# Tail scores and last-key value products of two head pairs in 64x64 quarters of TensorE's array

## The chip, the core and the metric

The kernel runs on one core of a Trainium2 chip. The metric is the device time of one execution in microseconds (us), as the median of several runs; lower is better. The engines are TensorE (PE, matmuls; PEld are its weight loads), VectorE (DVE), ScalarE (ACT), GpSimd (POOL) and SyncE (SP), which here issues nearly all DMAs from one queue in program order.

## What is computed

Attention of 8 sequences with 8 heads, 576 tokens and head size 64, in which weights below a threshold of the row's maximum are dropped, and behind it a feed-forward layer with an ELU, all in fp32:

```python
scores = scale * np.matmul(q, k.transpose(0, 1, 3, 2))          # (8, 8, 576, 576)
thresh = np.max(scores, axis=-1, keepdims=True) - tau
scores = np.where(scores >= thresh, scores, -1000000000.0)
attn = np.exp(scores - np.max(scores, axis=-1, keepdims=True))
attn = attn / (np.sum(attn, axis=-1, keepdims=True) + 1e-09)
x = np.matmul(attn, v)                                          # to (4608, 512)
h = x @ w_in                                                    # (4608, 2048)
g = np.where(h > 0.0, h, np.exp(np.minimum(h, 0.0)) - 1.0)
out = g @ w_out                                                 # (4608, 512)
```

## The kernel before

**Pairs and steps.** The 64 heads are worked on as 32 pairs of heads, since two heads of 64 fill the 128 partitions. 576 tokens are 4 chunks of 128 (`NC = 4`, together `MAIN = 512`) and a tail of 64 (`TAIL`). A pair takes five steps: steps 0 to 3 handle 128 queries of both heads, step 4 (`i == NC`) handles the 64 tail queries of both heads at once. `steps` (line 529) lists all (pair, step). A step computes scores into PSUM (`scores`, line 220), their maximum (`max_of`), exponentials on ScalarE (`exp_of`), the thresholded weights with their sum (`mask_of`, VectorE) and the normalized weights `w` (`normalize`, GpSimd).

**Scores.** In a full step each head is one row half of the array: 64 rows, 128 columns, twice 288 keys. In the tail step both heads are one matmul with 128 rows: the tail queries stand in a block-diagonal tile `qd`, which `copy_q` (line 200) fills on GpSimd from `qT`.

**The turn of the weights.** The value product needs `w` with keys on partitions. `turn_squares` (line 375) turns squares of 32 on VectorE into `x`, and SyncE writes `x` to a DRAM tile `there` (line 393, four DMAs). `fetch` (line 397) reads it back in the turned order into `wTa` (steps 0 and 1) or `wTb` (steps 2, 3 and the tail; lines 401 and 403). `wTa` and `wTb` have one buffer each. Step n is turned while step n+1 runs and fetched while step n+2 runs. The nine chunks of a turned step are 4 of the first head, one that both heads share (the last 64 keys of each), and 4 of the second head.

**Values.** `values` (line 408) makes one half of a pair's output: part 0 from `wTa`, part 1 from `wTb`. First one matmul over the whole array for the last keys of both heads (line 416: block-diagonal `vd`, chunk `NC`), then eight with 64 columns each (line 420: `vm`, the two heads in the two column halves). They add up in `pv`, a tile of the one bank of pool `t`. `values_out` (line 424) copies `pv` on ScalarE to `xt`, the feed-forward layer's input, and the tail tokens to DRAM.

**The third stage.** From pair 9 on (`MIDDLE`, line 854) the stage in question runs: attention of one batch beside the feed-forward layer of the one before, which uses a scheme of seven block products in place of eight. PSUM holds three banks for it (pool `f`), two score buffers of two banks (pool `s`) and one bank of pool `t`. Its unit on TensorE is a quarter of four matmuls, `ffn_quarters` (line 1176). The program order of every engine comes from a planned clock: `on_pe` (line 918) puts a piece on TensorE and moves the clock by a planned cost; `at(t, f)` puts work of other engines at a planned time. The times are only a plan that sorts instructions, and on the chip every engine works through its own list in order and waits on semaphores.

**Order within a pair.** I call the position of a step in its pair its place. The loop at line 1235 does, for each place: the fetch of step n-2 (planned 1.5 us into the place), `softmax` of the step (line 1194), then quarters, values and quarters. `QUARTERS` (line 1233) gives 8, 6, 4, 6 and 4 quarters to places 0 to 4. Part 1 of the pair ahead follows the quarters of place 2, part 0 of the running pair those of place 4 (`values_of(*steps[n - 3])`). `softmax` also plans loads and turns of q and k for later pairs: VectorE turns the raw tile `qm` in place 0 (`prep_q`, line 192), after which four DMAs load k into the same buffer (line 176); place 2 turns k and loads q; place 3 loads v.

## Time and profile before

| quantity | value |
|---|---|
| median of three runs (lowest, highest) | 1368.72 us (1367.94, 1369.15) |
| profiled execution: span from first to last instruction | 1366.1 us |
| granted TensorE clock | 0.994 |
| scores of pair 10's and pair 30's place 0 | 345.2 and 1065.1 us |
| places 0 to 4 of the pair at 705.19 us | 8.28, 6.55, 7.81, 6.24, 7.03 us |
| share of the 16 DMA engines, 400 to 1,100 us | 86.3% |
| VectorE and GpSimd busy in that pair of 35.91 us | 32.74 and 24.45 us |

How to read the lines of the profile: a group names the source line, the engine, the operation, the tiles (output<-inputs), the shape, and how many there were; then busy time, mean ns of one, and idle time ahead of it. A timeline row gives the start in us from the span's start, the length of the merged run, and what ran. A DMA row on SPq is the time in which SyncE issued it; its landing is told apart. `64*128` are rows and columns of the array that a matmul uses. `sc` are scores, `pv` values, `f` the feed-forward banks. An fp32 matmul of the program shows as two records.

### The profile page before, as it was taken

What the parts mean: (1) busy time and instruction counts of PE and PEld (TensorE: products, weight loads), DVE (VectorE), ACT (ScalarE), POOL (GpSimd) and SP (SyncE); (2) the same over time, 40 slices, a digit from 0 to 9 for tenths busy, and PEclk for the clock granted to TensorE, in tenths of its full rate; (3) what the DMA queues carried; (4) which work ended last, traced back from release to release, by engine and by line L of the source; (5) the groups of instructions that cost most, each with busy time, mean ns of one, the idle gap of its engine ahead of it and who ended that gap; (6) DMA issues with size and microseconds to landing.
All of it is one profiled execution on the core that took longest, in us unless ns stands there. A gap on an engine that the chain in (4) does not pass through costs nothing.

```text
span 1366.1 us, 22394 instructions
## 1 busy us (share of the span) xinstructions
PE 1340.4 (98%) x6796; PEld 1008.9 (74%) x6796; DVE 1064.7 (78%) x2344; ACT 638.5 (47%) x1418; POOL 825.2 (60%) x1322
## 2 busy tenths in 40 slices
PE   8998999999999999999999999999999999999998
PEld 7665746747777777777777777777777777888886
DVE  6879895988888887888798978888898875445433
ACT  5777675226354445545453636363636452412320
POOL 4657673878657574757475747675675646525423
PEclk9999999999999999999999999999999999999999
DMA  5254451688888989798889888897889785412211
GB/s 116 59 108 137 132 151 43 198 247 256 237 251 239 260 229 259 206 267 247 230 234 263 236 238 241 245 269 203 245 225 266 218 258 155 135 59 66 93 59 31
DMA packets 316343, 259.84 MB, mean 190 GB/s; under 512 B 208320, under 2 KB 272320, under 8 KB 316224
## 3 DMA queue, kind: packets, MB, share of 16 engines
q1 hardware_dynamic: 313856, 258.13, 67.6%
q8 instruction: 54, 0.88, 0.3%
q10 hardware_dynamic: 2368, 0.30, 0.2%
q14 instruction: 65, 0.53, 0.1%
HBM read 167.84 MB, written 90.51 MB: 189 GB/s over the span
## 4 chain that ended last, share of the span: by engine, by line
PE 89%; DVE 4%; ACT 2%; POOL 2%; issue 1%; DMA 0%; ACTq 0%; DVEq 0%; POOLq 0%; SPq 0%
PE f L1110 28%; PE f L955 28%; PE sc L236 13%; PE pv L420 9%; PE f L507 3%; PE rt L306 3%; PE pv L416 3%; PE f L467 2%; DVE mx L276 1%; POOL w L272 1%; DVE w L296 1%; ACT e L287 1%; DVE wtop L142 0%; ACT wTa L322 0%; DVE wtop L137 0%
## 5 line engine op out<-in xcount | busy, mean ns | idle before, releaser
L272 POOL TENSOR_SCALAR w<-w,rs 128x576 f32<-128x576 f32 x288 | 248.4, 867 | 120.7 <-DVE rs L303 99.9
L276 DVE TENSOR_REDUCE mx<-sc 128x1 f32<-128x576 f32 x270 | 192.8, 750 | 89.0 <-PE sc L236 88.8
L296 DVE SCALAR_TENSOR_TENSOR w<-sc,th,e 128x576 f32<-128x576 f32 x270 | 212.8, 811 | 26.7 <-ACT e L287 10.0
L287 ACT ACTIVATE e<-sc,nb,keep 128x576 f32<-128x576 f32 x270 | 223.0, 831 | 9.2 <-POOL nb L612 0.7
L285 ACT ACTIVATE nb<-mx,nkeep 128x1 f32<-128x1 f32 x254 | 75.2, 296 | 256.4 <-DVE mx L276 256.4
L380 DVE STREAM_TRANSPOSE x<-w 128x512 f32<-128x512 f32 (+1 forms) x350 | 182.6, 568 | 8.2 <-POOL w L272 8.2
L236 PE MATMUL sc<-kT,qT 64*128 64x288 f32 x1024 | 166.7, 431 | 9.0 <-DVE w L296 6.1
L236 PEld LDWEIGHTS sc<-kT,qT 64*128 64x128 f32 x1024 | 92.8, 187 | 71.4 <-issue 49.4
L280 POOL TENSOR_SCALAR th<-mx,ntau 128x1 f32<-128x1 f32 x270 | 75.7, 281 | 114.0 <-DVE mx L276 113.3
L955 PE MATMUL f<-xt,sw 128*128 128x256 f32 x512 | 128.9, 389 | 0.5 <-DVE g L977 0.5
L955 PE MATMUL f<-xt,w_in_sb 128*128 128x256 f32 x512 | 124.5, 382 | 0.3 <-ACT w L969 0.2
L955 PEld LDWEIGHTS f<-xt,sw 128*128 128x128 f32 x512 | 93.3, 190 | 28.9 <-issue 13.5
L955 PEld LDWEIGHTS f<-xt,w_in_sb 128*128 128x128 f32 x512 | 96.1, 190 | 18.9 <-ACT xs L432 4.6
L1110 PE MATMUL f<-w_out_sb,s 128*128 128x256 f32 x448 | 109.4, 387 | 0.0
L1110 PE MATMUL f<-w_out_sb,g 128*128 128x256 f32 x448 | 107.6, 382 | 0.5 <-DVE g L1010 0.5
L1110 PE MATMUL f<-t,s 128*128 128x256 f32 x448 | 106.6, 380 | 0.3 <-POOL s L1047 0.3
L955 PE MATMUL f<-x,w_in_sb 128*128 128x256 f32 x448 | 105.8, 379 | 0.0
L1110 PEld LDWEIGHTS f<-w_out_sb,s 128*128 128x128 f32 x448 | 82.3, 190 | 23.0 <-issue 11.3
L1110 PEld LDWEIGHTS f<-w_out_sb,g 128*128 128x128 f32 x448 | 83.8, 190 | 16.9 <-issue 4.2
L974 POOL TENSOR_TENSOR u<-u,w 128x256 f32<-128x256 f32 x64 | 48.9, 764 | 76.5 <-ACT u L969 76.5
L1110 PEld LDWEIGHTS f<-t,s 128*128 128x128 f32 x448 | 84.1, 190 | 13.7 <-POOL s L1047 2.7
L955 PEld LDWEIGHTS f<-x,w_in_sb 128*128 128x128 f32 x448 | 85.1, 190 | 11.6
(165 smaller groups left out, 2435.4 us busy)
## 6 DMA issues: line engine op xcount, KB each, us to landing
there<-x SPq DMA_DIRECT2D x500, 144.0 KB, 4.2
wTb<-there SPq DMA_DIRECT2D x75, 576.0 KB, 4.9
wTa<-there SPq DMA_DIRECT2D x50, 576.0 KB, 4.3
sw<-win_sums SPq DMA_DIRECT2D x62, 384.0 KB, 4.6
t<-wout_sums SPq DMA_DIRECT2D x45, 512.0 KB, 5.6
qm<-in_q_dram SPq DMA_DIRECT2D x128, 72.0 KB, 4.2
vm<-in_v_dram SPq DMA_DIRECT2D x64, 128.0 KB, 4.3
wst<-in_moe_w_in_dram SPq DMA_DIRECT2D x16, 512.0 KB, 4.3
```

The source lines that it names most:

```text
L236: nc.tensor.matmul(scs[h][:, a, :HALF], qs[r], kT[r, k0 : k0 + HALF], start=True, stop=True)
L272: nc.gpsimd.tensor_scalar(wv, wv, st["rs"][:, h : h + 1], 1.0, ALU.mult, ALU.mult)
L276: nc.vector.tensor_reduce(st["mx"][:, h : h + 1], st[h][:, :, :HALF], axis=AX.XY, op=ALU.max)
L280: nc.gpsimd.tensor_scalar(st["th"][:, h : h + 1], st["mx"][:, h : h + 1], 1.0, ntau, ALU.mult, ALU.add)
L285: nc.scalar.mul(st["nb"][:, h : h + 1], st["mx"][:, h : h + 1], nkeep)
L287: nc.scalar.activation(e, st[h][:, :, :HALF], AF.Exp, bias=st["nb"][:, h : h + 1], scale=keep)
L296: nc.vector.scalar_tensor_tensor(wv, sc[:, :, :HALF], st["th"][:, h : h + 1], e, ALU.is_ge, ALU.mult, accum_out=st["sm"][:, h : h + 1])
L380: nc.vector.transpose(x[:, :, c0 : c0 + nc_], src.rearrange("p (c g n) -> p g c n", c=nc_, n=T))
L420: nc.tensor.matmul(pv[h * D : (h + 1) * D, g0 * T : g1 * T], vm[:, h, c], wT[:, g0:g1, h * (NC + 1) + c], start=False, stop=(c == NC - 1), ...
L955: nc.tensor.matmul(loc["banks"][place], left[:, j], right[:, j], start=(begins and j == 0), stop=(j == 1), skip_group_check=True)
L974: nc.gpsimd.tensor_tensor(loc[name], x(), loc[other], op)
L1110: nc.tensor.matmul(place(m), lhs, rhs, start=(begins and v == 0), stop=(v == RU - 1), skip_group_check=True)
```

## The change

From pair 9 on (`JOINED`), the steps of a pair run in the order 0, 1, tail, 2, 3, so the tail stands in place 2. In that place a new function, `tails_and_values`, issues two things together: the tail scores of the running pair, as four matmuls of 64 rows and 64 columns (each head on its own, without `qd`), and the last-key products of the pair ahead, also as four 64x64 matmuls, two for each half of the output. The four positions of the array are shared so that in each round head 0's scores, head 0's last keys, head 1's scores and head 1's last keys have one quarter each. The remaining products of both parts (`values_main`) follow at once, and then the place's quarters. `pv` is now a tile of two banks from the score pool `s`. The values of the last pair come by themselves at the end (`last_values`).

The tail's turn now has five chunks for each head instead of nine for both: one turn of 128x512 and two of 64 keys for two chunks, four writes, and two reads instead of one. `copy_q` is no longer called in this stage. The fetch in place 2 is planned at 3.4 us instead of 1.5. `QUARTERS` becomes 7, 6, 2, 7 and 6, all behind the values.

```diff
--- before.py
+++ after.py
@@ -308,10 +308,10 @@
 
 
     def turned_tile(pr, i):
-        if i in (0, 2):
-            n = (2 if i == 0 else 3) * NT
-            wTs[pr, i // 2] = wtp.tile([P, n, NCH, T], FP32, name="wTb" if i else "wTa")
-        return wTs[pr, min(i // 2, 1)], i % 2 * NT + (NT // 2 if i >= 2 else 0)
+        part = int(i >= 2)
+        if (pr, part) not in wTs:
+            wTs[pr, part] = wtp.tile([P, (2 + part) * NT, NCH, T], FP32, name="wTb" if part else "wTa")
+        return wTs[pr, part], i % 2 * NT + (NT // 2 if part else 0)
 
 
     def turn_parts(pr, i):
@@ -383,6 +383,19 @@
             turn_part(0, w[:, :MAIN], NC)
             turn_part(NC, w[:, MAIN : MAIN + P], 1)
             turn_part(NC + 1, w[:, MAIN + P :], NC)
+        elif pr >= JOINED:
+            turn_part(1, w[:, :MAIN], NC)
+            tail = w[:, MAIN:S].rearrange("p (g n) -> p g n", n=T).unsqueeze(1).broadcast_to([P, 2, 2, T])
+            for g in (0, 2):
+                nc.vector.transpose(x[:, g : g + 2, :: NC + 1].rearrange("p g c n -> p c g n"), tail)
+            there = turns[pr, i] = dram.tile([NT, T, NT, (NC + 1) * T], FP32, name="there")
+            for p in range(NT):
+                h = int(p < 2)
+                nc.sync.dma_start(
+                    there[:, :, (p + 2) % NT].rearrange("c k n -> k c n"),
+                    x[p * T : (p + 1) * T, :, 1 - h : NC + 2 - h].rearrange("k c j n -> k c (j n)"),
+                )
+            return
         else:
             turn_part(0, w[:, :MAIN], NC)
             turn_part(NC + 1, w[:, :MAIN], NC)
@@ -399,6 +412,13 @@
         wT, g0 = turned_tile(pr, i)
         if i < NC:
             nc.sync.dma_start(wT[:, g0 : g0 + NT].rearrange("p g c n -> p g (c n)"), back)
+        elif pr >= JOINED:
+            for h in range(2):
+                g = h * (3 * NT - 2)
+                nc.sync.dma_start(
+                    wT[:, g : g + 2, h * NC : h * NC + NC + 1].rearrange("p g c n -> p g (c n)"),
+                    back[:, 2 * h : 2 * h + 2],
+                )
         else:
             nc.sync.dma_start(
                 wT.rearrange("p (a b) c n -> p a b (c n)", b=2)[:, ::5],
@@ -421,6 +441,46 @@
                                  start=False, stop=(c == NC - 1), skip_group_check=True)
         return lambda: values_out(pr, part, pv)
 
+    def tails_and_values(pr, before):
+
+        pv = parts = None
+        if pr is not None:
+            qT, kT, _ = pairs[pr]
+            st = open_steps[pr, NC] = {x: small.tile([P, 2], FP32, name=x) for x in ("mx", "nb", "th", "sm", "rs")}
+            sc = st[0] = psum["s"].tile([P, 2, 512], FP32, name="sc")
+        if before is not None:
+            b, j = divmod(before, NPAIR)
+            vm, vd = (raws[before][x] for x in ("vm", "vd"))
+            parts = [wTs.pop((before, part)) for part in range(2)]
+            if b not in xts:
+                xts[b] = xpool.tile([P, KJ, MAIN], FP32, name="xt")
+            pv = psum["s"].tile([P, 2, 512], FP32, name="pv", tag="sc")
+
+        def span(h, part):
+            return (2 * h, 2 * h + 10) if part else (0, 2 * NT)
+
+        for a in range(2):
+            for h in range(2):
+                r, x = slice(h * D, (h + 1) * D), a ^ h
+                if pr is not None:
+                    nc.tensor.matmul(sc[D - h * D : P - h * D, x, :HALF], qT[r, MAIN:],
+                                     kT[r, TAIL + x * HALF : TAIL + (x + 1) * HALF], start=True, stop=True,
+                                     skip_group_check=True)
+                if before is not None:
+                    g0, g1 = span(h, x)
+                    nc.tensor.matmul(pv[r, x, g0 * T : g1 * T], vd[r, r], parts[x][r, g0:g1, NC],
+                                     start=True, stop=False, skip_group_check=True)
+
+        def values_main(part):
+            for c in range(NC):
+                for h in range(2):
+                    g0, g1 = span(h, part)
+                    nc.tensor.matmul(pv[h * D : (h + 1) * D, part, g0 * T : g1 * T], vm[:, h, c],
+                                     parts[part][:, g0:g1, h * (NC + 1) + c], start=False, stop=(c == NC - 1),
+                                     skip_group_check=True)
+
+        return values_main, [lambda part=part: values_out(before, part, pv[:, part]) for part in range(2)]
+
     def values_out(pr, part, pv):
         b, j = divmod(pr, NPAIR)
         q0, n = TAIL * part, (3 if part else 2) * NT * T
@@ -526,8 +586,9 @@
 
     NP = B * NPAIR
     NB = NC + 1
-    steps = [(pr, i) for pr in range(NP) for i in range(NB)]
     per_seq = NPAIR * NB
+    JOINED = (2 * NPAIR + 1)
+    steps = [(pr, i) for pr in range(NP) for i in ((0, 1, NC, 2, 3) if pr >= JOINED else range(NB))]
 
     def behind(pr, i):
         if i in (1, NB - 1):
@@ -1191,10 +1252,20 @@
 
         begun = [0.0]
 
-        def softmax(pr, i):
-            hs = heads_of(i)
+        def softmax(n):
+            pr, i = steps[n]
+            hs, place = heads_of(i), n % NB
             t = begun[0] = clock[0]
-            on_pe(1.25, lambda: scores(pr, i, hs))
+            if i == NC:
+                loc = {}
+                before = pr - 1 if pr > JOINED else None
+                on_pe(1.35, lambda: loc.update(zip(("main", "outs"), tails_and_values(pr, before))))
+                if before is not None:
+                    for part, cost in enumerate((1.8, 2.3)):
+                        end = on_pe(cost, lambda: loc["main"](part))
+                        at(end + 0.1, loc["outs"][part])
+            else:
+                on_pe(1.25, lambda: scores(pr, i, hs))
             turn_at = t + 1.25 + 0.72 * len(hs)
             for h in hs:
                 at(t + 1.2 + 0.01 * h, lambda h=h: max_of(pr, i, h))
@@ -1203,7 +1274,7 @@
                 at(t + (2.1 if i < NC else 2.3) + 1.05 * h, lambda h=h: exp_of(pr, i, h))
                 at(turn_at + 1.6 + 0.85 * h, lambda h=h: mask_of(pr, i, h))
             if i or pr:
-                at(turn_at, lambda: turn_squares(*steps[pr * NB + i - 1]))
+                at(turn_at, lambda: turn_squares(*steps[n - 1]))
             m = turn_at + 1.6 + 0.85 * len(hs)
             at(m, lambda: reciprocal_of(pr, i, hs))
             at(m + 0.1, lambda: run_elus(m))
@@ -1211,51 +1282,59 @@
                 at(m + 0.2 + 0.7 * h, lambda h=h: normalize(pr, i, [h]))
             for x in (2.8, 3.8, 5.0):
                 at(t + x, lambda: run_extra(max(0.9, extra[0][0])) if extra else None)
-            if pr + 1 < NP and i in (0, 2):
-                at(m + 0.2, lambda: (prep_k if i else prep_q)(pr + 1))
-                at(m + 1.3, lambda: (copy_k if i else copy_q)(pr + 1))
-
-            if pr + 1 < NP and i == 0 and pr * NB > MIDDLE:
+            if pr + 1 < NP and place in (0, 2):
+                at(m + 0.2, lambda: (prep_k if place else prep_q)(pr + 1))
+                if place:
+                    at(m + 1.3, lambda: copy_k(pr + 1))
+
+            if pr + 1 < NP and place == 0 and n > MIDDLE:
                 at(m + 0.9, lambda: load(pr + 1, ("km",), True))
-            if pr + 2 < NP and i == 2:
+            if pr + 2 < NP and place == 2:
                 at(m + 0.9, lambda: load(pr + 2, ("qm",), True))
-            if pr + 1 < NP and i == 3:
+            if pr + 1 < NP and place == 3:
                 at(m + 0.9, lambda: load(pr + 1, ("v",)))
 
         def values_of(pr, i):
-            if i in (1, NB - 1):
+            if i in (1, NB - 1) and pr < JOINED:
                 loc = {}
                 part = 0 if i == 1 else 1
                 end = on_pe(3.1 if part else 2.3, lambda: loc.update(out=values(pr, part)))
                 at(end + 0.1, lambda: loc["out"]())
 
 
-        QUARTERS = ((4, 4), (4, 2), (4, 0), (4, 2), (4, 0))
+        def last_values():
+            main, outs = tails_and_values(None, NP - 1)
+            for part in range(2):
+                main(part)
+            for out_ in outs:
+                out_()
+
+        QUARTERS = (7, 6, 2, 7, 6)
         group(1)
         for n in range(MIDDLE, len(steps) + 3):
-            pr, i = divmod(n, NB)
+            pr, place = divmod(n, NB)
             if n <= len(steps) + 1:
-                at(clock[0] + 1.5, lambda n=n: fetch(*steps[n - 2]))
+                at(clock[0] + (3.4 if place == 2 else 1.5), lambda n=n: fetch(*steps[n - 2]))
             if 0 < n - MIDDLE < 4:
                 x = n - MIDDLE - 1
                 at(clock[0] + 5.0, lambda x=x: nc.sync.dma_start(wout_sums[0, x], out_sums[x].rearrange("p u n -> p (u n)")))
             if n == MIDDLE + NB:
                 ges.append((raw.tile([P, S // T, T], FP32, name="km").rearrange("p j d -> p (j d)")[:, : 2 * CT], lambda: None))
             if n == len(steps):
-                at(clock[0], lambda: turn_squares(*steps[-1]))
+                at(clock[0] + 2.0, lambda: turn_squares(*steps[-1]))
             if n < len(steps):
-                softmax(*steps[n])
+                softmax(n)
             b = pr // NPAIR
-            if n < len(steps) and pr % NPAIR == 0 and i == 3 and b > 1:
+            if n < len(steps) and pr % NPAIR == 0 and place == 3 and b > 1:
                 xs = [late["x"].tile([P, 2, CT], FP32, name=f"x{x}") for x in range(3)]
                 jobs = sums_x(b - 1, xs)
                 for x, f in enumerate(jobs):
                     at(clock[0] + 4.2 + 0.5 * x + (4.0 if x > 2 else 0), f)
                 group(b - 1)
-            before, behind_ = QUARTERS[i]
-            ffn_quarters(before)
+            if n == len(steps) + 2:
+                on_pe(5.0, last_values)
+            ffn_quarters(QUARTERS[place])
             values_of(*steps[n - 3])
-            ffn_quarters(behind_)
         attending[0] = False
         xs = [late["x"].tile([P, 2, CT], FP32, name=f"x{x}") for x in range(3)]
         for x, f in enumerate(sums_x(B - 1, xs)):
```

## The prediction

> **What bounds the kernel now.** First the page: the busy row and the slices of TensorE, then the chain that ended last.
>
> ```profile
> PE 1340.4 (98%) x6796; PEld 1008.9 (74%) x6796; DVE 1064.7 (78%) x2344; ACT 638.5 (47%) x1418; POOL 825.2 (60%) x1322
> PE   8998999999999999999999999999999999999998
> PE 89%; DVE 4%; ACT 2%; POOL 2%; issue 1%; DMA 0%; ACTq 0%; DVEq 0%; POOLq 0%; SPq 0%
> ```
>
> TensorE has work in every slice and carries 89% of the chain. In the changed stage (309 to about 1,165 us) a pair takes 36.0 us ((1065.1 - 345.2) / 20 pairs), the same in all pairs to 0.1 us. A microsecond taken from TensorE's queue is a microsecond of time, and so is each microsecond that it waits.
>
> Next the matmul groups by form in 400 to 1,100 us, for the groups that the change touches.
>
> ```profile
> L236 PE MATMUL sc<-kT,qT 64*128 64x288 f32 x616 | 95.5, 429 | 0.0
> L420 PE MATMUL pv<-wTb,vm 128*64 128x320 f32 x320 | 47.5, 439 | 0.0
> L236 PE MATMUL sc<-kT,qd 128*128 128x288 f32 x80 | 22.7, 406 | 0.0
> L416 PE MATMUL pv<-wTb,vd 128*128 128x384 f32 x40 | 16.2, 486 | 0.0
> L416 PE MATMUL pv<-wTa,vd 128*128 128x256 f32 x40 | 11.9, 379 | 0.0
> ```
>
> Each written matmul is two records, and a record's 379 to 486 ns includes pipeline latency. Costs must therefore be read as distances between starts, in TensorE's timeline of one pair:
>
> ```profile
> 713.47 1.24 PE L236 MATMUL sc<-kT,qT 64*128 64x288 f32 x8
> 714.64 1.99 PE L1110 MATMUL f<-w_out_sb,s 128*128 128x256 f32 x8
> 716.47 1.89 PE L1110 MATMUL f<-w_out_sb,g 128*128 128x256 f32 x8
> 720.02 1.24 PE L236 MATMUL sc<-kT,qT 64*128 64x288 f32 x8
> 724.79 0.81 PE L416 MATMUL pv<-wTb,vd 128*128 128x384 f32 x2
> 725.53 2.37 PE L420 MATMUL pv<-wTb,vm 128*64 128x320 f32 x16
> 727.83 0.51 PE L236 MATMUL sc<-kT,qT 64*128 64x288 f32 x2
> ```
>
> Two quarters (8 records) take 1.73 us, so one is 0.864. A scores group takes 1.17 (713.47 to 714.64). The first two quarters behind it take 1.83, 0.1 more: the switch back to the whole array. Sixteen half-array value records take 2.30, about half of sixteen in a row.
>
> Last SyncE, whose queue carries the turn of the weights through DRAM, in the same pair and in the next one (scores of place 0 at 705.19 and 741.11).
>
> ```profile
> 708.98 0.34 SPq L401 DMA_DIRECT2D wTb<-there  x1
> 710.07 1.93 SPq L393 DMA_DIRECT2D there<-x  x4
> 713.78 1.94 SPq L176 DMA_DIRECT2D qm<-in_k_dram  x4
> 715.89 0.57 SPq L403 DMA_DIRECT2D wTb<-there  x1
> ...
> 749.76 3.97 SPq L176 DMA_DIRECT2D qm<-in_k_dram  x4
> 754.19 1.14 SPq L403 DMA_DIRECT2D wTb<-there  x1
> ```
>
> ```profile
> DMA to landing us min/median/max: 4.1/5.0/6.7
> SPq L401 <- DMA there<-x: 99.8, 60, 5.1
> ```
>
> The first of these is the L403 read-back alone, the second the longest wait of SyncE in 16 pairs. The read-back of 715.89 is needed at 724.79, so today 8.9 us cover a landing of about 5. In 21 pairs this read-back landed 14.8 to 19.0 us after the scores of place 0, mean 16.8. The change removes most of that cover.
>
> **What the Trainium skill says.** "TensorEngine Tiling (Array Packing)", Tiling Modes, says that tiles of the array work in parallel and that changing the mode drains TensorE. The trace agrees for two tiles (16 records in 2.30 us) and for the drain (about 0.1 us). "TensorE: Matmul & The Clock Gate", Part 3, says that row and column packing compose (10.6 times with 16 tiles), and that matmuls keep program order; no run here shows four tiles yet. "DMA: Bandwidth & Descriptors", Anatomy of one DMA, says that a semaphore is waited for on the issuing sequencer, not in the DMA engines. The trace agrees: SyncE stands 99.8 us at L401, and what is queued behind stands too.
>
> **The change part by part.**
>
> *TensorE.* Removed per pair: tail scores 0.97 us (734.29 to 735.26), part 0 of the values 2.40 (702.79 to 705.19), part 1 3.04 (724.79 to 727.83): 6.41. These include the switches from values to scores. Added: the joint block. Each quarter gets four passes of 288 columns on average (scores twice 288, values 256 and 320), which is what each half gets in a normal scores group, so 1.17 if all four run at once. Then part 0's main products 1.72 and part 1's 2.16 (the spans above without their end switch). Switches: 0.1 into the block, 0.15 out to the quarters and 0.1 for their first load, and 0.09 for each of the two scores groups that now follow a quarter instead of values: 0.53. Sum 5.58. Gain 0.83 us a pair, say 0.85. If quarters run only two at a time the block is 0.96 longer and the gain is -0.1. I take four: the trace has two row tiles at once and two column tiles at once, each with its own moving data.
>
> There are 22 joint blocks with values (pairs 10 to 31): -18.7 us. Pair 9 has only tail scores, in two quarters: +0.2.
>
> *The new deadline.* The values of the pair ahead now stand at the start of place 2, in front of its quarters. From the scores of place 0 to the block are 14.83 us today (705.19 to 720.02) less one quarter (7 instead of 8): 13.97. The last read-back for the block is that of the step in place 4, turned in place 0, issued in place 1. It keeps its place on SyncE behind the four loads of k, which wait for VectorE's turn of qm (ends 713.75, loads from 713.78). In the light pair: issue 10.7 after place 0, landing 4.9 later, 15.6, so 1.6 late. In the heavy pair: 13.1 plus 5.3 is 18.4, 4.4 late. The mean of 16.8 is 2.8 late. The wait stands in TensorE's queue ahead of the second half of tail scores, the values and everything behind; nothing covers it.
>
> *What eases it.* The tail step's turn moves 5 of 9 chunks: 1,152 KB out and back become 640, of 8.7 MB a pair (169.08 MB in 19.5 pairs), -5.9% on engines that are 86% busy. VectorE loses one 128x512 turn (about 0.6 us) and ScalarE and GpSimd next to nothing; the two 64x64 copies on GpSimd go. Place 4 now holds a full step, so its turn comes without the fourth instruction, perhaps 0.4 us earlier. A pair that waits also lets the queue drain. Against this stand two reads for the tail instead of one. I bound the mean wait by 0 and 2.8 and take half, 1.4 us.
>
> *Moved read-back.* The one of place 2 (planned at 3.4 instead of 1.5) waits for part 0's products, for wTa has one buffer. They end about 1.17 + 1.72 = 2.9 us into the place; behind it on SyncE stand loads of q and v with more than 10 us of room. Nothing. Quarters and their follow-up work only change places: 28 a pair before and after.
>
> *End.* After the last scores 13 quarters (11.2 us) come before the last values, 18 (15.6) before. The chain there (turn 2.0 + 1.5, four writes 2, landing 4.2, read 4.9) is 14.6 without traffic delay, less what the empty queues save. I take a wait of 2.5 and a gain of 0.5: +2.0.
>
> Sum: 22 x (1.4 - 0.85) = +12.1, +0.2, +2.0 = +14.3 on the span of 1366.1: 1380.4. The median of the runs lies 2.6 above that span, so 1383.0.
>
> **Rivals.**
>
> *The read-back lands in time (faster).* If VectorE turns qm a microsecond earlier, the k loads leave earlier and the writes' landing (9.2 to 9.9 in light pairs) sets the issue: 10.0 + 4.0 is 14.0, the deadline. Decided at landing 13.97; break-even at 14.8. With no wait: -18.7 + 0.2 + 2.0 = -16.5, 1352. For it: less traffic, and step 0's read-back of today lands in light pairs 12.2 after its scores, with no loads before it. Against: not one of 21 read-backs in this place landed before 14.8.
>
> *Quarters run two at a time.* 0.96 more in 22 blocks: +21, about 1404. The two-tile evidence speaks against it.
>
> *The score buffers.* pv now takes the second of two score buffers, and scores of place 3 need it. Between the last product and them lie two quarters, 1.8 us; result latency 0.25 and three copies (0.37 + 0.42) need 1.0. ScalarE started such a copy 1.7 us late once (705.26 to 706.94). At such a lag each time 0.9 us are lost: with half of that in all pairs +10, 1393.
>
> *Smaller waits.* With a mean wait of 0.85 the two cancel and nothing can be told; 0.2%, 2.7 us, is about what a measurement here can tell from no change.
>
> **How the numbers follow.** Wait at the joint block 0.62 (of that 0.06 within 0.2%), in time 0.19, two at a time 0.09, buffers 0.10. Faster 0.19, same 0.06, slower 0.75. The likeliest one's own range is 1370 to 1402. The range to state goes from 1355 (most of the faster case is left with waits in a few heavy pairs) to 1404.
>
> **What would show it.** Right: an idle gap of TensorE of 1 to 2 us in front of the joint block's values, released by the read-back of wTb, larger in pairs with first products than in those with second ones, and a pair period of 36.5. Four records of the block starting within some 20 ns confirm the gain. Wrong: a period of 35.1 with no gap; or a block of 2.1 us; or a gap at the scores of place 3 released by ScalarE.

## The result, and the profile after

The changed kernel takes 1434.98 us (four runs, 1431.25 to 1435.13); the kernel before took 1368.93 beside it. The ratio is 1.0478, 95% interval 1.0464 to 1.0493. The sign of the prediction held, by luck as will be seen. Its 1383.0 and its range up to 1404 did not: 66 us were lost, not 14. The profiled execution spans 1433.2 us.

The page of the changed kernel, with the rows shown of before: busy time, slices of TensorE, the chain that ended last.

```profile
PE 1356.1 (95%) x6980; PEld 1008.3 (70%) x6980; DVE 1065.2 (74%) x2325; ACT 640.3 (45%) x1418; POOL 816.7 (57%) x1274
PE   9989999999989999999999999989999998999998
PE 62%; DVE 13%; DMA 9%; POOL 6%; issue 4%; ACT 3%; SPq 3%; DVEq 0%; ACTq 0%; POOLq 0%
```

VectorE, ScalarE and GpSimd have no more to do than before (1065, 640 and 817 us against 1065, 639 and 825). Yet TensorE's share of the chain fell from 89% to 62%, and what it lost went mostly to VectorE (4 to 13%), DMA (0 to 9) and GpSimd (2 to 6). No engine got more work; the work comes too late. The waits of TensorE's matmuls from 300 to 1,240 us say for what (us in all, times, longest):

```profile
PE f L1171 <- DVE g L1071: 40.7, 25, 4.3
PE pv L471 <- DMA wTb<-there: 9.7, 7, 2.2
PE sc L236 <- DVE w L296: 1.7, 5, 0.4
```

In the kernel before the longest sum in this view is 0.5 us. The second row is the wait that was predicted. The first is four times as large and was in no case of the prediction: a matmul of the feed-forward layer's second product (L1171) waits for `g`, the ELU of the first one (L1071).

The view shows less than a wait costs. Matmul records start 0.216 us apart and are shown 0.379 long, so 0.16 us of each wait are hidden beneath the record ahead of it, and the first record after a wait is followed by the next one 0.320 us later instead of 0.216. That makes some 0.27 us more for each wait.

**Where that wait stands.** The layer's quarters come in rounds: 28 of a first product (`first_product`), then 28 of `second_round` that read its results `g`. A quarter is two matmuls of the program, four records (not four matmuls, as the section on the kernel before says). A round is one pair long, so every second pair begins with the change from first to second. Here is the timeline of the kernel before at such a change. The last quarter of the first product ends at 702.8:

```profile
702.79 0.59 PE L416 MATMUL pv<-wTa,vd 128*128 128x256 f32 x2
703.94 0.73 POOL L974 TENSOR_TENSOR t<-g,u 128x256 f32<-128x256 f32 x1
704.71 0.42 DVE L977 TENSOR_TENSOR g<-f,t 128x256 f32<-128x256 f32 x1
705.19 1.24 PE L236 MATMUL sc<-kT,qT 64*128 64x288 f32 x8
705.23 0.63 ACT L988 ACTIVATE ge<-g 128x512 f32<-128x512 f32 x1 [2.68 <-DVE g L977]
705.89 0.63 ACT L993 ACTIVATE ge<-ge 128x512 f32<-128x512 f32 x1
706.36 1.99 PE L1110 MATMUL f<-w_out_sb,g 128*128 128x256 f32 x8
706.55 0.69 DVE L1010 SCALAR_TENSOR_TENSOR g<-ge,g 128x512 f32<-128x512 f32 x1 [0.31 <-ACT ge L993]
```

A chain runs from the first product's last quarters to the last ELU that the second round needs at its start: product `t` on GpSimd, add on VectorE, exponential and minus one on ScalarE, ELU on VectorE, done at 707.24, 4.45 us after the last quarter. Part 0 of the values (2.40) and a scores group (1.17) lie over it, and the quarter that needs it comes second. Its second matmul is the first to read the new ELU, the seventh of the eight records at 706.36; a narrower window shows it:

```profile
707.76 0.38 PE L1110 MATMUL f<-w_out_sb,g 128*128 128x256 f32 x1
```

So the chain had 0.5 us of slack under 5.0 us of cover, of which the values were 2.40. The same change in the changed kernel:

```profile
726.83 1.24 PE L236 MATMUL sc<-kT,qT 64*128 64x288 f32 x8
726.86 0.72 POOL L1108 TENSOR_TENSOR s<-g 128x256 f32<-128x256 f32 x1
727.03 1.09 DVE L1071 SCALAR_TENSOR_TENSOR g<-ge,g 128x512 f32<-128x512 f32 x1
727.54 1.17 POOL L1035 TENSOR_TENSOR t<-g,u 128x256 f32<-128x256 f32 x1
728.05 1.21 DVE L1071 SCALAR_TENSOR_TENSOR g<-km,g 128x512 f32<-128x512 f32 x1
729.18 0.41 DVE L1038 TENSOR_TENSOR g<-f,t 128x256 f32<-128x256 f32 x1
729.68 0.63 ACT L1049 ACTIVATE ge<-g 128x512 f32<-128x512 f32 x1 [3.53 <-DVE g L1038]
730.34 0.63 ACT L1054 ACTIVATE ge<-ge 128x512 f32<-128x512 f32 x1
731.17 0.68 DVE L1071 SCALAR_TENSOR_TENSOR g<-ge,g 128x512 f32<-128x512 f32 x1
731.91 0.70 PE L1171 MATMUL f<-w_out_sb,g 128*128 128x256 f32 x2 [1.90 <-DVE g L1071]
```

The values are gone from this spot (they follow the joint block of place 2), and the chain is 5.0 us long: two older ELUs stand ahead of the add, and block sums (L1108) ahead of `t`. TensorE idles 1.90 us. In nine of the eleven changes it idles 2.36 to 2.37. In every one another ELU is late 11 to 13 us further on, in place 1, by 0.8 to 1.2 us. Of the 40.7 us, 25.3 stand at the change, 10.2 in place 1 and 5.2 at the end of the stage.

Behind most gaps of 2.37 us a second loss follows. The view by stretches after the change at 809.2 (us, busy time and instructions of PE, PEld, DVE, ACT, POOL, clock, DMA share, GB/s):

```profile
810.00:812.00 2.00, 2.00 (x6) 1.65 (x5) 1.35 (x3) 1.67 (x4) 1.55 (x3) 0.50 0.29 62
816.00:820.00 4.00, 4.00 (x22) 3.18 (x21) 3.15 (x7) 2.06 (x4) 3.23 (x7) 1.00 0.61 90
```

TensorE runs at half its clock for 3.4 us. After the same gap of 2.37 us, place 0 lasts 11.73 us with such a stretch and 10.04 without (pairs at 650.1 and 573.0): 1.7 us each, and there are nine in the stage (eight behind waits for ELUs, one behind a read-back), and a double one at its end.

**What the block itself does.** TensorE's timeline of an unhindered joint block:

```profile
744.84 0.45 PE L466 MATMUL sc<-kT,qT 64*64 64x288 f32 x1
744.85 0.43 PE L471 MATMUL pv<-wTa,vd 64*64 64x256 f32 x1
744.85 0.45 PE L466 MATMUL sc<-kT,qT 64*64 64x288 f32 x1
744.86 0.48 PE L471 MATMUL pv<-wTb,vd 64*64 64x320 f32 x1
...
745.97 1.95 PE L478 MATMUL pv<-wTa,vm 128*64 128x256 f32 x16
747.75 2.32 PE L478 MATMUL pv<-wTb,vm 128*64 128x320 f32 x16
750.00 1.13 PE L1171 MATMUL f<-t,s 128*128 128x256 f32 x4
```

Four records start within 20 ns and the block takes 1.13 us (predicted 1.17). The shortest lengths of the five places, 7.41, 6.55, 7.09, 7.41 and 6.55, make 35.0 us for a pair without waits, against 36.0: the gain of some 0.85 us a pair is there, rather 1.0, so some 21 us in 22 pairs. With its waits a pair takes 39.0 us on average (scores of place 0 at 339.9 and, 21 pairs later, at 1158.7).

### The profile page after: what moved, and what is told of

It is laid out like the page before. It is cut to its first block, busy times and chain, and to the rows that moved or that the text cites. A ratio compares the mean times of both kernels' runs of the same rounds, so it can differ in the third digit from the quotient of the medians.

```text
span 1433.2 us, 22711 instructions
## 1 busy us (share of the span) xinstructions
PE 1356.1 (95%) x6980; PEld 1008.3 (70%) x6980; DVE 1065.2 (74%) x2325; ACT 640.3 (45%) x1418; POOL 816.7 (57%) x1274
## 4 chain that ended last, share of the span: by engine, by line
PE 62%; DVE 13%; DMA 9%; POOL 6%; issue 4%; ACT 3%; SPq 3%; DVEq 0%; ACTq 0%; POOLq 0%
PE f L1171 19%; PE f L1016 16%; PE sc L236 8%; PE pv L478 6%; DVE mx L276 3%; PE rt L306 3%; DVE x L380 3%; DMA wTb<-there 3%; PE f L527 3%; DMA there<-x 2%; PE f L567 2%; PE pv L440 2%; POOL s L1108 2%; DVE g L1071 2%; DMA wTa<-there 1%
## 5 line engine op out<-in xcount | busy, mean ns | idle before, releaser
L272 POOL TENSOR_SCALAR w<-w,rs 128x576 f32<-128x576 f32 x288 | 241.3, 842 | 156.6 <-DVE rs L303 139.1
L236 PE MATMUL sc<-kT,qT 64*128 64x288 f32 x1024 | 175.9, 431 | 9.5 <-DVE w L296 7.8
L380 DVE STREAM_TRANSPOSE x<-w 128x512 f32<-128x512 f32 (+1 forms) x327 | 167.4, 559 | 0.0
L280 POOL TENSOR_SCALAR th<-mx,ntau 128x1 f32<-128x1 f32 x270 | 82.5, 307 | 147.5 <-DVE mx L276 146.4
L1171 PE MATMUL f<-w_out_sb,g 128*128 128x256 f32 x448 | 115.8, 393 | 40.7 <-DVE g L1071 40.7
L236 PEld LDWEIGHTS sc<-kT,qT 64*128 64x128 f32 x1024 | 99.5, 187 | 69.9 <-issue 49.0
L1171 PEld LDWEIGHTS f<-w_out_sb,g 128*128 128x128 f32 x448 | 84.2, 194 | 65.5 <-DVE g L1071 50.7
L1016 PE MATMUL f<-xt,w_in_sb 128*128 128x256 f32 x512 | 121.1, 379 | 0.5 <-ACT w L1030 0.5
L1171 PE MATMUL f<-t,s 128*128 128x256 f32 x448 | 113.5, 387 | 1.2 <-DVE s L1108 0.7
L1016 PE MATMUL f<-x,w_in_sb 128*128 128x256 f32 x448 | 109.0, 382 | 0.0
L1171 PE MATMUL f<-w_out_sb,s 128*128 128x256 f32 x448 | 108.8, 382 | 0.0
L1171 PEld LDWEIGHTS f<-t,s 128*128 128x128 f32 x448 | 82.1, 190 | 26.4 <-issue 8.2
L1171 PEld LDWEIGHTS f<-w_out_sb,s 128*128 128x128 f32 x448 | 84.2, 190 | 15.2 <-issue 4.2
```

Source lines behind the costliest of these rows:

```text
L236: nc.tensor.matmul(scs[h][:, a, :HALF], qs[r], kT[r, k0 : k0 + HALF], start=True, stop=True)
L272: nc.gpsimd.tensor_scalar(wv, wv, st["rs"][:, h : h + 1], 1.0, ALU.mult, ALU.mult)
L280: nc.gpsimd.tensor_scalar(st["th"][:, h : h + 1], st["mx"][:, h : h + 1], 1.0, ntau, ALU.mult, ALU.add)
L380: nc.vector.transpose(x[:, :, c0 : c0 + nc_], src.rearrange("p (c g n) -> p g c n", c=nc_, n=T))
L1016: nc.tensor.matmul(loc["banks"][place], left[:, j], right[:, j], start=(begins and j == 0), stop=(j == 1), skip_group_check=True)
L1171: nc.tensor.matmul(place(m), lhs, rhs, start=(begins and v == 0), stop=(v == RU - 1), skip_group_check=True)
```

## The experiments

Times are medians; each ratio is to runs of the kernel before on the same chip (1366.0 to 1368.5). In the lines of the experiments line numbers are up to three higher than in the changed kernel.

| run | median, us | ratio (95% interval) |
|---|---|---|
| e1_cover_gone | 1399.85 | 1.0235 (1.0214 to 1.0255) |
| e8_order_alone | 1413.39 | 1.0343 (1.0318 to 1.0367) |
| e15_order_and_cover | 1428.93 | 1.0452 (1.0434 to 1.0469) |
| e12_order_no_scaling | 1383.60 | 1.0105 (1.0082 to 1.0129) |
| e13_order_short_max | 1401.99 | 1.0239 (1.0217 to 1.0262) |
| e10_order_shift | 1418.41 | 1.0359 (1.0326 to 1.0392) |
| e9_block_in_two | 1432.61 | 1.0467 (1.0419 to 1.0515) |
| e4_k_behind | 1420.72 | 1.0387 (1.0356 to 1.0418) |
| e2_round_order | 1422.71 | 1.0402 (1.0379 to 1.0425) |
| e3_shifted | 1420.86 | 1.0404 (1.0375 to 1.0432) |
| e5_shift_and_k | 1406.37 | 1.0296 (1.0257 to 1.0335) |
| e6_more_in_2 | 1414.54 | 1.0345 (1.0308 to 1.0382) |
| e7_sums_on_pool | 1417.50 | 1.0384 (1.0358 to 1.0410) |
| e11_light_place | 1437.71 | 1.0500 (1.0470 to 1.0529) |
| e14_after_short_max | 1409.50 | 1.0297 (1.0271 to 1.0323) |
| e16_after_no_scaling | 1432.37 | 1.0449 (1.0410 to 1.0487) |
| e17_sums_later | 1425.11 | 1.0406 (1.0380 to 1.0433) |
| e18_sums_and_k | 1408.83 | 1.0308 (1.0286 to 1.0330) |

**The cover alone.** The kernel before, with two of place 4's quarters put behind the values, so that these no longer stand between the last first-product quarter and the second round:

```diff
-QUARTERS = ((4, 4), (4, 2), (4, 0), (4, 2), (4, 0))
+QUARTERS = ((4, 4), (4, 2), (4, 0), (4, 2), (2, 2))
```

> The kernel before, with one edit: in place 4 two quarters stand ahead of part 0's values and two behind them, instead of four ahead. No tail moved, no 64x64 block. Theory (lost cover): at the change from a first product to a second round, which falls on the start of place 0, TensorE had values and scores (3.6 us) between the last quarter of the one and the first of the other; now it has scores alone (1.2 us), so TensorE waits there for VectorE's last ELU (line 1010): 1.5 to 3 us and sometimes half clock at 11 changes, +20 to +50 us, 1389 to 1419. Rival (places 3, 4 and 0 all hold full steps in the changed kernel, so VectorE is late): here place 4 keeps its light tail step, so no wait over 0.5 us and no more than +5 us, at most 1374.

1399.85, as the theory said: 31 us for moving two quarters. The waits for ELUs in its stage, 0.5 us in the kernel before:

```profile
PE f L1110 <- DVE g L1010: 18.4, 23, 4.4
```

They are shorter than the theory's 1.5 to 3 us (0.6 to 0.7), but come twice in each change, as in the changed kernel, and none but the last, of 4.4 us, is followed by the half clock. Some 4 of the 31 us are not cover: place 4 takes 7.02 us instead of 6.82 in nearly all pairs, since the values now part its quarters in two. (The tail scores of the pair at 705.19 begin at 734.29, so that places 3 and 4 take 6.46 and 6.82 us; the table ahead parts them at 734.07.)

**The order alone.** The kernel before with only the order 0, 1, tail, 2, 3; tail scores, values, turn and quarters by place stay as they were (`MOVED` is pair 9):

```diff
-steps = [(pr, i) for pr in range(NP) for i in range(NB)]
+steps = [(pr, i) for pr in range(NP) for i in ((0, 1, NC, 2, 3) if pr >= MOVED else range(NB))]
```

> The kernel before with only the order of steps of the changed one (0, 1, tail, 2, 3 from pair 9 on): old tail scores, old turn, values and quarters where they stood, so part 0's values still cover the change of round at place 0, but place 4 holds a full step. Theory (the lost cover is the greater part): waits for line 1071 of at most 1 us a change, +0 to +15 us, 1369 to 1384. Rival (four full places in a row make VectorE late): +30 us and more, above 1399.

1413.39: the theory fell, for the order by itself costs 47 us, as the rival's number said. Its waits are others; ELUs are late only once:

```profile
PE f L1172 <- POOL s L1109: 14.7, 23, 1.3
PE sc L236 <- DVE w L296: 10.5, 16, 0.8
```

Its timeline shows how one of the first kind comes about:

```profile
655.97 0.17 DVE L303 RECIPROCAL rs<-sm 128x2 f32<-128x2 f32 x1
656.32 1.02 POOL L272 TENSOR_SCALAR w<-w,rs 128x576 f32<-128x576 f32 x1 [0.94 <-DVE rs L303]
657.31 0.72 POOL L1109 TENSOR_TENSOR s<-s,g 128x256 f32<-128x256 f32 x1
658.08 1.13 PE L1172 MATMUL f<-t,s 128*128 128x256 f32 x4 [1.12 <-POOL s L1109]
```

The sum that TensorE needs stands in GpSimd's queue behind the scaling of weights, which waits for VectorE's reciprocal. Four full steps in a row, which the rival names, are not new: the kernel before has them in places 0 to 3. But its light tail step stood right ahead of place 0, and the second round's block sums fell into the first full step. Now the full steps fill places 3, 4, 0 and 1, and these sums fall into the third of them.

**Which engine.** Two ways to take work from the order-alone kernel. First, GpSimd's scaling left out for full steps (the weights stay unscaled):

```diff
     def normalize(pr, i, hs):
         st = open_steps[pr, i]
+        if pr >= MOVED and i != NC:
+            return
```

> The kernel with the new order alone (1413.4), with GpSimd's scaling of the weights by rs left out for the four full steps of each pair from the tenth on: 8 multiplications of 0.74 us, 5.9 us of GpSimd a pair, are missing (the weights stay unscaled). Theory (VectorE sets the pace of four full steps in a row; GpSimd is late only because its queue stands at a scaling whose sum VectorE has not delivered): the waits on GpSimd's sums (18.4 us, 23 times) go, those on the masks of VectorE (13.1 us, 16) stay: 1392 to 1400. Rival (GpSimd itself is the bound): both go, for masks are late behind elus that wait for GpSimd's products: 1372 to 1385.

Second, the maximum of full steps over 32 columns of each half instead of 288 (the rest is left out of the maximum):

```diff
-nc.vector.tensor_reduce(st["mx"][:, h : h + 1], st[h][:, :, :HALF], axis=AX.XY, op=ALU.max)
+n = 32 if pr >= MOVED and i != NC else HALF
+nc.vector.tensor_reduce(st["mx"][:, h : h + 1], st[h][:, :, :n], axis=AX.XY, op=ALU.max)
```

> The kernel with the new order alone (1413.4), with the maximum of the four full steps of each pair from the tenth on taken over 32 of 288 columns of each half only: some 0.6 us of VectorE less for each of 8 maxima, 4.4 us a pair (the rest of the scores is left out of the maximum). Theory (VectorE sets the pace): both kinds of waits go, 1372 to 1388. Rival (GpSimd is the bound): the masks' waits go at most, those on GpSimd's sums stay, 1395 to 1410.

1383.60 and 1401.99: both in the rival's range. Without the scaling the waits on sums fall from 14.7 to 2.6 and those on masks from 10.5 to 4.0; with less VectorE work the sums still cost 14.1. What the order costs is settled mostly in GpSimd's queue, where the scaling that was left out had also stood waiting for VectorE; some 15 us stay without it.

The same two edits in the changed kernel, the shortened maximum and then the missing scaling (each leaves out what it left out above):

> The changed kernel (1435) with the same shortened maximum of the full steps: 4.4 us of VectorE a pair are missing. Theory (at the change of round the wait is the length of one chain from the last quarter of the first product to its elu, some 4.5 us, and the cover of 2.4 us is gone, so load on VectorE is only part of it): some 15 to 30 us less, 1405 to 1420. Rival (VectorE's load is all of it): 1355 to 1390, near the 1350 of no waits.

> The changed kernel (1435) without GpSimd's scaling of the full steps: 5.9 us of GpSimd a pair are missing. Theory (the chain at the change of round runs through GpSimd's products s, u and t, but its length is set by VectorE's and ScalarE's parts; the turns leave a little earlier): 1415 to 1430. Rival (GpSimd is the bound): 1355 to 1390.

1409.50, in the theory's range, and 1432.37, just above it. Here GpSimd's load does nothing that can be told: the ELU waits stay at 41.4. Less VectorE work brings 25, of which the half clock is 15: its trace has no such stretch in the stage, where the changed kernel has nine. But 31.1 of the 40.7 us of ELU waits stay. The wait at the change of round is mostly the length of a chain; VectorE's load adds to it.

**Do the two costs add?** The order alone with e1's `QUARTERS`:

> The kernel with the new order alone (1413.4), with two of the four quarters of place 4 put behind part 0 of the values instead of all four ahead of it, as e1_cover_gone did to the kernel before (+31). Theory (the two costs are different waits and add; the joint block then gives back some 21 and its late read-back takes 14, which makes the changed kernel's 1435): 1435 to 1450. Rival (both are the same lateness of the softmax engines at the change of round, counted twice): 1410 to 1425.

1428.93, between theory and rival: +61 where +47 and +31 would add to +78. So they overlap by some 17. Its ELU waits are 30.0 us and the sums' 8.0. All this without a single 64x64 matmul.

**The predicted wait.** The changed kernel with the loads of k planned in place 1, behind the read-back that the joint block needs:

```diff
-if pr + 1 < NP and place == 0 and n > MIDDLE:
-    at(m + 0.9, lambda: load(pr + 1, ("km",), True))
+if pr + 1 < NP and place == 1 and n > MIDDLE + 1:
+    at(t + 2.0, lambda: load(pr + 1, ("km",), True))
```

> The changed kernel, with one edit: the four loads of k are planned in place 1, behind the read-back of wTb, instead of in place 0 ahead of it. Theory: only the waits of the joint block for the read-back go (10.9 us in 7 pairs, with half-clock stretches up to 20 us): 1415 to 1428, and the waits for line 1071 stay near 45 us. Rival (SyncE's late read-backs are what delays everything): more than -40 us, below 1395.

1420.72, as the theory said: the read-back waits fall from 9.7 to 0.7 us, and 14 us are won. The mechanism of the prediction is real and is at most a fifth of the loss. Part of the 14 is the half clock, which its trace shows four times in the stage instead of nine, though the gaps of 2.36 us are still there.

**Shortening or moving the wait for ELUs.** Four edits of the changed kernel. The second round's quarters in the order 0, 2, 6, 1, 3, 4, 5, so that the last ELU is needed later:

```diff
-if (f, a) == (second_round, (B, 1)):
+if (f, a) == (second_round, (B, 1)) or attending[0] and f is second_round:
```

> The changed kernel, with one edit: the first seven quarters of each second round come in the order 0, 2, 6, 1, 3, 4, 5, as the program already has for its last one, so that three quarters instead of one precede the first that needs the newest hidden units. Theory (lost cover): 1.7 us of the wait in place 0 is covered in 11 changes, and half of its half-clock stretches go: -19 to -37 us, 1398 to 1416. Rival (late read-backs of wTb make the loss): within 5 us of 1435.

1422.71, between theory and rival: ELU waits fall to 16.9, but waits for adds (7.3) and copies (7.0) come up.

The first 13 places of the stage one quarter shorter, so that the change of round falls on the joint block, whose 5 us would cover the chain:

```diff
-ffn_quarters(QUARTERS[place])
+ffn_quarters(QUARTERS[place] - int(n < MIDDLE + 13))
```

> The changed kernel, with one edit: each of the first 13 places has one quarter less, so that from pair 12 on the change from first product to second round falls on the joint block in place 2 (5.1 us of TensorE's work) instead of on the start of place 0. Theory (lost cover): the waits for line 1071 go but for the first two pairs, with their half-clock stretches: -45 to -57 us, 1378 to 1390. Rival (VectorE late because places 3, 4, 0 and 1 are all full): its waits stay in another place, no more than -15 us.

1420.86, far above the theory's 1390 and with a gain of 14 us inside the rival's: the ELU waits go (4.8), as they should, but read-backs of `wTb` (12.3) and masks (8.6) are now late instead.

Block sums of place 4 planned 4.6 us later, so that they no longer stand ahead of `t` in GpSimd's queue; the other engines' lists keep their order:

```diff
-for x in (2.8, 3.8, 5.0):
+for x in (7.4, 8.4, 9.4) if place == 4 and pr >= JOINED else (2.8, 3.8, 5.0):
```

> The changed kernel (1435) with the block sums of place 4 asked for 4.6 us later, so that in GpSimd's queue the three sums of 0.72 us no longer stand ahead of the product t of the last quarter of the first product; the order of VectorE and ScalarE is as in the changed kernel, and nothing is left out. Theory (the wait at the change of round is one chain, copy, product t on GpSimd, add, exponential, minus one, elu, and its length comes from what stands ahead of it in the queues): t starts 1.4 us sooner, the waits for elus fall from 44.7 to 20 to 32 us and some of the half-clock stretches behind them go: 1408 to 1422. Rival (the two elus of the part ahead on VectorE, 727.0 to 729.2, set the adds anyway, or the late sums make TensorE wait instead): 1428 to 1440.

1425.11, between theory and rival. In its profiled run, the fastest of the four (1417.95), the ELU waits fall from 40.7 to 31.0, somewhat less than the theory said, and the postponed sums cost 5.9. Its timeline shows what holds the chain now (the last quarter ended at 719.4):

```profile
718.83 0.72 POOL L1035 TENSOR_TENSOR t<-g,u 128x256 f32<-128x256 f32 x1 [0.71 <-ACT g L1083]
719.70 0.99 DVE L1071 SCALAR_TENSOR_TENSOR g<-ge,g 128x512 f32<-128x512 f32 x1
720.61 0.68 DVE L1071 SCALAR_TENSOR_TENSOR g<-km,g 128x512 f32<-128x512 f32 x1
721.21 0.41 DVE L1038 TENSOR_TENSOR g<-f,t 128x256 f32<-128x256 f32 x1
723.93 0.48 PE L1171 MATMUL f<-w_out_sb,g 128*128 128x256 f32 x1 [1.77 <-DVE g L1071]
```

`t` is done at 719.55, but the add waits in VectorE's list behind two older ELUs: the rival's mechanism. The chain is 4.5 us, as in the kernel before, and TensorE still idles: so most of what is left there is the missing cover.

**Combinations.** The shift with the later k loads (the edits of e3 and e4); the same with three quarters in place 2 and six in place 3; and the same again with two of each batch's input sums on GpSimd for batches 2 to 6:

```diff
-        QUARTERS = (7, 6, 2, 7, 6)
+        QUARTERS = (7, 6, 3, 6, 6)
```

```diff
+        pp = nc.gpsimd.tensor_tensor if 1 < g < B - 1 else tt
-                lambda: tt(b12, b12, b22, ALU.subtract), lambda: tt(xs[2], b21, b22, ALU.add),
-                lambda: tt(b21, b21, b11, ALU.subtract)]
+                lambda: pp(b12, b12, b22, ALU.subtract), lambda: tt(xs[2], b21, b22, ALU.add),
+                lambda: pp(b21, b21, b11, ALU.subtract)]
```

> The changed kernel with both edits of the third and the fourth run: the change of round shifted to the joint block, and the k loads behind the read-back. Theory (two separate losses, a lost cover and a late read-back): the shifted kernel's waits for DMA (14.5 and some 9 us more that the profile puts down to issue and to writes) go, its scores still wait for masks in place 2 (10 us): 1385 to 1398. Rival (VectorE late in four full places in a row sets the pace whatever else is mended): within 8 us of 1421.

> As the run with both edits, and the quarters of the places are 7, 6, 3, 6, 6 instead of 7, 6, 2, 7, 6: 0.86 us more between the values and the scores of place 3, which wait there for a mask. Theory: the 10 us of waits of scores for masks go for the greater part, -5 to -11 us against that run, 1375 to 1390. Rival (VectorE sets the pace): the wait moves to another place, within 3 us of that run.

> As the run before in this list, and two of the five block sums of a batch's input (five batches of 8) are made on GpSimd instead of VectorE, 1.3 us less on VectorE in places 3 and 4 of one pair in four. Theory: places 4 and 0 of these pairs lose about 1.9 us today; half of it comes back, -3 to -6 us. Rival: GpSimd, busy two thirds, delays what follows there, no gain.

1406.37, 1414.54 and 1417.50. The first lies between theory and rival and is, with e18 below, the fastest found that has the new order and computes everything; in its profiled run, the slowest of the four, the waits sit at the joint block (20.2 us) and at masks (7.5). The other two missed their theories' gains and only moved the waits (masks 11.3 and 9.3).

Later sums with later k loads:

> The same with the k loads behind the read-back in place 1, as in e4_k_behind (1420.7). Theory (the two waits are independent, so both gains add): 1393 to 1409. Rival (the sums bring nothing): 1416 to 1426.

1408.83, at the edge of the theory's range: the gains of e17 and e4 (10 and 14) add to the 26 seen, as those of different waits would.

Two tries to find a better spot for the change of round, in the order-alone kernel behind place 2 and in the changed kernel with place 2 rearranged (block, three quarters, main products, one quarter) and the later k loads. The cores of the two edits:

```diff
-            ffn_quarters(before)
+            ffn_quarters(before - int(n < MIDDLE + 18))
```

```diff
-        QUARTERS = (7, 6, 2, 7, 6)
+        QUARTERS = (7, 6, 3, 6, 5)
...
-            ffn_quarters(QUARTERS[place])
+            ffn_quarters(QUARTERS[place] - int(n < MIDDLE + 16))
+            if mains:
+                main_values()
+            if place == 2:
+                ffn_quarters(1)
```

> The kernel with the new order of steps alone, and 18 places with one quarter less at its start, so that the change from first product to second round falls behind place 2, which holds the light tail step, four quarters and part 1's values, just as it fell behind such a place in the kernel before. Theory (what matters is that the light step and the values stand right ahead of the change of round): the waits of the second round go, 1366 to 1380. Rival (four full steps in a row cost it wherever the change of round falls): above 1400.

> The changed kernel put together by the same rule: in place 2 the joint block, three quarters, the main products of both parts, one quarter; quarters 7, 6, 4, 6, 5; k loads behind the read-back; 16 places with one quarter less at the start, so that the change of round falls between the third quarter of place 2 and the main products. Theory: no wait of the second round, and the block's gain of 0.98 us a pair shows against waits for the read-back and for masks of some 0.5 us: 1350 to 1372. Rival (four full steps in a row cost it anyway): above 1390.

1418.41 and 1437.71: both theories fell. Sums (12.5) and `wTa` (7.8) wait in the first, masks (16.9) and adds of the first product (16.3) in the second. The first of them has the light step right ahead of the change of round again, as the kernel before has, and still loses 51 us; so that neighbourhood is not all that the order broke. None of the spots tried was free, and no version beat the kernel before.

**The block's own order.** In the changed kernel, the four tail-score matmuls all ahead of the four last-key products:

```diff
+        for a in range(2):
+            for h in range(2):
+                r, x = slice(h * D, (h + 1) * D), a ^ h
                 if before is not None:
```

> The changed kernel, with one edit: in the joint block all tail scores come first and then all last-key products, so that in program order only two quarters of the array stand next to each other. Theory (the block's gain is that four quarters run at once, because they alternate): the block takes 1.9 to 2.1 us instead of 1.13 where it doesn't wait, and a pair 0.8 to 1.0 us more: 1449 to 1457. Rival (TensorE starts a quarter's work as soon as that quarter is free, whatever stands ahead of it): block within 0.3 us of 1.13, time within 8 us of 1435.

1432.61, no slower than the changed kernel. TensorE's timeline:

```profile
748.95 0.46 PE L466 MATMUL sc<-kT,qT 64*64 64x288 f32 x2
748.97 0.43 PE L474 MATMUL pv<-wTa,vd 64*64 64x256 f32 x1
748.98 0.48 PE L474 MATMUL pv<-wTb,vd 64*64 64x320 f32 x1
749.24 0.40 PE L466 MATMUL sc<-kT,qT 64*64 64x288 f32 x1
...
750.09 1.95 PE L481 MATMUL pv<-wTa,vm 128*64 128x256 f32 x16
```

The first value records start at 748.97, before the second scores of either head, which stand ahead of them in the program. The block takes 1.14 us, and the rival was right.

## Why the prediction was wrong, point by point

- *The step that failed* is in "Moved read-back", the edits that were costed at nothing: "Quarters and their follow-up work only change places: 28 a pair before and after." It counted them on TensorE and asked of no other engine what stood over its chains; the new order of the steps has no term for the other engines' queues at all. The runs put in its place: +47 for the order of the steps alone, +31 for the cover alone, +61 for both.
- The view that would have shown it was open before: the ELU that ends at 707.24, the matmul that reads it at 707.76. A single wait of 0.5 us at L1110 in the whole stage looked like room. There was room for 0.5 us, and 2.40 us of cover were taken away.
- *The sign* held by luck. The predicted terms alone, as measured, are -21 for the block, at most +14 for the read-backs (e4) and some +3 for the end without its ELU wait: a kernel some 4 us faster. It is slower through costs that the prediction put at nothing.
- *TensorE* was right: four quarters at once, 1.13 us, a gain of 1.0 us a pair (predicted 0.85).
- *The new deadline* and *What eases it*: right in mechanism, wrong in size. The waits are 9.7 us in 7 blocks, not 1.4 us in each of 22 (31 us). With what follows on them they cost 14 (e4).
- *End*: +2.0 predicted. From the last scores group to the end of the span it is 245.4 us (1187.8 to 1433.2) against 235.9 (1130.2 to 1366.1): +9.5. The ELU wait of 4.3 us that ends at 1201.1 and the half clock behind it, up to 1205.3 (half of 4.2 us lost, 2.1), make most of it.
- The rivals: quarters two at a time is refuted by the block's length. The score buffers are not seen; waits at scores are 1.7 us in all. None of the rivals looked beyond TensorE and DMA.

The sum from the runs: order and cover +61 (e15), block -21, late read-back +14, which makes +54 of +66. Some 5 of the other 12 us are half clock. With the one at its end (2.1 us), the stretches cost the changed kernel 17 us; e15, with one in the stage and 2.5 us at its end, 4; e4, with four and 2.0, 9. So 13 us come in between e15 and the changed kernel, of which e4's 14 already hold 9. No run removed the stretches by themselves, and the rest was not taken apart. The trace of the changed kernel alone gives a sum close to the measured one, as an estimate: 54 us of waits in the view of 300 to 1,240 us, 0.27 more for each of the 42 (11), and 17 of half clock make 82, less the block's 21 are 61.

Left open: whether a new plan of all queues for the order 0, 1, tail, 2, 3 could keep the block's 21 us. The edits tried moved one queue at a time, and each handed the wait on. No run has the block with the old order either, so its 21 us are read from the lengths of places.

## What to carry to other kernels

Work on the bounding engine that doesn't wait for a chain is the chain's cover: before moving it, list which chains on other engines run beneath it, and their slack, above all where one phase feeds the next. A busy share of 47 to 78% on the helper engines, as in the kernel before, says nothing about this; look for the instruction that ends just before it is needed. And a light step among heavy ones is where the helpers catch up: moving it cost 47 us here, and no edit that moved the work of one queue won them back.

## What the hardware showed that was not expected

- Matmuls in different quarters of the array start out of the program's order (e9). "TensorE: Matmul & The Clock Gate", Part 3, says that matmuls start and end in strict program order; between tiles this measurement says otherwise, and it decides. A wait does hold what is behind it: in the block at 780.9 the second round of tail scores started only at 782.7, with the values that had waited for `wTb`.
- The half clock came after idle gaps of TensorE as short as 1.9 us. In the changed kernel's stage it followed seven of nine gaps of 2.36 to 2.37 us and one of two at 1.9; in e17 none of nine gaps of 1.60, but one of 1.58. Part 1 of that page names an idle window of about 3.4 us; here gaps well below it were enough, though not each time. The trace of the changed kernel shows which: its nine stretches begin at 345.2, 423.7, 502.2, 655.8, 809.4, 939.1, 966.4, 1044.9 and 1123.4, whole multiples of 3.413 us apart, each behind one such interval in which TensorE idled 1.87 us or more, and none behind an interval with 1.69 or less. A gap of 2.37 us that falls astride the border of two (those before 578.2 and 885.7) has no stretch behind it. In other runs the least idle time is not so sharp.
- The same ELU on VectorE took 0.68 us or 1.09 and 1.21, and the same pair of scalings on GpSimd 1.46 or 2.41. "GPSIMD Engine Reference", Key points, says that the two share their interfaces to SBUF and contend where VectorE reads two inputs from it, as the ELU does. In the changed kernel's stage, all 39 ELUs beside which GpSimd worked over 0.15 us on operations of two tiles took 1.04 to 1.21 us; of the other 57, 51 took at most 0.70. In the kernel before 14 of the 54 ELUs beside such work took at most 0.70 as well, and no run isolated it.
